# Row maxima of attention pairs 1 to 7 in two parts, spread differently over the first steps

## The chip, the core and the metric

The kernel runs on one core of one Trainium2 chip. The metric is the device time of one execution in microseconds (us), the median of several runs. Five engines work side by side on a core and meet only through semaphores: PE (TensorE, matmuls into PSUM), DVE (VectorE), ACT (ScalarE), POOL (GpSimd) and SP (SyncE), which here does nothing but issue DMAs. Each engine runs its own list of instructions strictly in order: an instruction that waits holds back all that stand behind it on the same engine.

## The reference, cut to what matters

```python
def _attn_ref(q, k, v):                       # 8 batches, 8 heads, 1152 positions, 64 wide
    q_pool = q.reshape(B, H, S // 2, 2, D).mean(axis=3)
    scores = scale * np.matmul(q_pool, k.transpose(0, 1, 3, 2))
    scores = scores - np.max(scores, axis=-1, keepdims=True)
    attn = np.exp(scores)
    attn = attn / (np.sum(attn, axis=-1, keepdims=True) + 1e-09)
    return np.matmul(attn, v)

def _moe_ref(x, modality_id, w_gate, modality_bias, w1, w2):   # 4608 tokens, 8 experts
    logits = x @ w_gate + modality_bias[modality_id]
    e_idx = np.argmax(logits, axis=1)
    ...                                       # softmax weight of the chosen expert
    for e in range(E):
        h = np.maximum(x[mask] @ w1[e], 0.0)
        out[mask] = gate_w[mask, None] * (h @ w2[e])
```

The attention output is the input of the mixture of experts. The change lies in the attention alone.

## The kernel before, in words

**Pairs and steps.** The 64 heads are worked two at a time: 32 pairs, which the code and this text number p = 0 to 31 (the "pairs 2 to 8" of the change's title are p = 1 to 7). A pair takes NSTEP = 18 steps, so the attention is one loop over 576 steps t in `attention`; then `experts` runs the expert blocks. The order of instructions on each engine is exactly the order in which this loop writes them (a manual schedule). ORD says in which order a step writes its parts: "s" writes one bank of scores (432 columns: a product with B1 at L1051, one with B2 at L1052, then the exponential on ACT at L1053), "v" one chunk of the products of probabilities with values (L1110 to L1112), "M" one piece of the row maxima, "X" extra pieces of the row maxima by a rule, "F" and `ends` what was put off to this step.

**Row maxima.** The softmax needs the largest score of each query before the exponentials. `maxpass(p)` makes rough products of queries (tile QB) and keys (tile hi) for this alone: for each of 9 blocks of 128 queries two products of 512 keys (L984), each followed by a `tensor_reduce` on DVE (L985), and for every four blocks one product of the last 128 keys (L992, L993). A PSUM tile `pm` holds a product until DVE has reduced it; there are three. That makes 18 L984 products and 21 pieces per pair. `row` then takes the maximum of the parts (DVE, L935, tile m), turns it with PE (L949) into a row, scales it (DVE, L958, tile mr) and copies it by a DMA of SP (L959) into row D of B2, where the score products (L1052) pick it up as one more term. In a pair the first head (j = 0, the pair's steps 0 to 8) needs queries 0 to 575 and the second head (j = 1, steps 9 to 17) queries 576 to 1151. A pair in TWO_ROWS sends its maxima as two rows, blocks 0 to 4 and blocks 5 to 8, and its first head waits for the first of them only; other pairs send one row of 9 blocks ahead of their first step.

**How many pieces.** `mxq` is the queue of started maxima. M takes one piece per step. X takes three per step while t < T_F, one per step while t < X_ALL = 8, and after that one in every step with t % X_IN == 0 or whenever two pairs stand in the queue (every fourth step from t = 105 on).

**Queues around it.** SP issues, in program order, the loads of raw queries, keys and values (L756, L757, L761), the copies that place a pair's operands (L739: QB, B1, B2), the rows (L959), the zero rows of B2 (L1209) and the transposes of finished outputs (L1094). A DMA's semaphore is one of eight that SP uses in turn. POOL makes sums and casts of queries (L771, L780, tile qh), low parts (L818, tile lo), high parts of values (L911 to L918, VH) and, from p = 4 on, issues the DMA that loads the keys cast to f16 (L795 in `load_hi`, tile hi). The load of pair p + 3's raw queries and keys (`load_kq`) and the transposes of outputs (`turns`) are issued in `put`, right behind the row that ends with block 8.

Of the kernel before, what the change touches and what calls it, by code (L numbers as in the profile page):

```python
# [40 lines left out]
NSTEP = 2 * NKC  # L41
# [19 lines left out]
T_RT = (20, 35, 43, 61)  # L61
D2 = (1, 0, 0, 0, 3)
T_K2 = 0
T_F = 7
T_P2 = 1
T_P1 = 8
T_M1 = 5
# [4 lines left out]
T_CAST = -36  # L72
# [2 lines left out]
T_PLACE = -17  # L75
T_REST = -13
ST = 2
T_LV = (-24, -34, -36)
VS0 = 4
V1 = (9, 11, (14, 15), 18, (18, 19))  # L80
LOWS0 = (((0, 1152, 'A', 2), (1152, 1728, 'D', 3)),)
# [65 lines left out]
ORD = ('NvJMvsvMsvXF', 'JvvsMvvXFvv', 'vFvvsJvXv')  # L147
FIRST = (0, 1)
T_PRE = 1
TWO_ROWS = (1,)  # L150
X_ALL = 8
X_SOME = 105
X_IN = 3
T_MX2 = -23
T_MX3 = -23
FIN = 0
# [541 lines left out]
def attention(tc, ctx, att, ident, npairs, xpool, on_two, on_split, on_scale, jobs, side, set_pm, started, ahead, hip, own_port):  # L698
# [39 lines left out]
    def move(o, i):  # L738
        nc.sync.dma_start(out=o, in_=i)  # L739
# [35 lines left out]
    def split_qh(p):  # L775
        s = st[p]
        qh = s["qh"]
        made.add((p, "qh"))
        if p > 1:
            (nc.gpsimd if QH_POOL else nc.vector).tensor_copy(qh, s["q"][:, 0:SQ])  # L780
        else:
            nc.scalar.copy(qh, s["q"][:, 0:SQ])
        if p > 1:
            place_qb(p)

    def place_qb(p):
        qh = st[p]["qh"]
        for j in range(2):
            r = slice(j * D, (j + 1) * D)
            move(QB[p % 2].rearrange("p u n -> p (u n)")[r, j * SQ:(j + 1) * SQ], qh[r])  # L790
# [140 lines left out]
    def row(p, mp, u0, u1):  # L931

        n = u1 - u0
        m9 = sm.tile([P, 9], F32, name="m9")
        nc.vector.tensor_reduce(m9[:, 0:n], mp[:, u0:u1], op=ALU.max, axis=AX.X, negate=True)  # L935

        def first_row():
            nc.vector.tensor_scalar(first_m[:, :, D], m9[:, 0:n], 1.0 / ROW, 16.0 * math.log(PSC) / ROW, op0=ALU.mult, op1=ALU.add)
            for v0, v1, pt, copy in ((0, 3, small(), nc.scalar.copy), (3, n, some(0), nc.vector.tensor_copy)):
                for v in range(v0, v1):  # L940
                    nc.tensor.matmul(pt[0:D + 1, (v - v0) * P:(v - v0 + 1) * P], first_m[:, v], ident16, start=True, stop=True, skip_group_check=True)
                copy(B2[0][D:D + 1, 2 * S + v0 * P:2 * S + v1 * P], pt[D:D + 1, 0:(v1 - v0) * P])
            made.add((p, f"row{u1}"))

        def finish():
            if p == 0 and u0 == 0:
                return first_row()
            pt = some(0) if p else small()
            nc.tensor.transpose(pt[0:n, 0:P], m9[:, 0:n], ident)  # L949
            if now[0] > NSTEP:  # L950
                later_end(FD, lambda: put(pt))
            else:
                put(pt)

        def put(pt):
            mr = sm.tile([9, P], F16, name="mr", bufs=1)
            made.add((p, f"row{u1}"))
            nc.vector.tensor_scalar(mr[0:n], pt[0:n, 0:P], 1.0 / ROW, 16.0 * math.log(PSC) / ROW, op0=ALU.mult, op1=ALU.add)  # L958
            nc.sync.dma_start(out=B2[p % 2][D:D + 1, 2 * S + u0 * P:2 * S + u1 * P], in_=mr[0:n])  # L959
            if ahead and p == npairs - 1:  # L960
                for i in FIRST:
                    ahead[2](i, room[i])
            while turns:
                turns.pop(0)()
            if ahead and p == npairs - 1:
                for i in range(len(FIRST), NF):
                    ahead[2](i, room[i])
            if 0 < p < npairs - 3 and u1 == 9:
                load_kq(p + 3)
        return finish  # L970

    def maxpass(p, mp=None):

        s = st[p]
        need(p, *(("qh", "hi0", "hi1") if p else ()))
        u0 = 0 if mp is None else 5
        two = p in TWO_ROWS
        rest = []
        if mp is None:
            mp = sm.tile([P, 9, 3], F32, name="mp")  # L980
        for u in range(u0, 9):
            for t in range(2):
                pm = ps_max.tile([P, 512], F32, name="pm")
                nc.tensor.matmul(pm, QB[p % 2][:, u], s["hi"][:, t * 512:(t + 1) * 512], start=True, stop=True)  # L984
                nc.vector.tensor_reduce(mp[:, u, t:t + 1], pm, op=ALU.max, axis=AX.X)  # L985
                yield
            rest.append(u)
            if len(rest) == 4 or u == 8 or two and u == 4:
                n = len(rest)
                pm = ps_max.tile([P, 512], F32, name="pm")[:, 0:n * P].rearrange("p (n k) -> p n k", n=n)  # L990
                for i, v in enumerate(rest):
                    nc.tensor.matmul(pm[:, i], QB[p % 2][:, v], s["hi"][:, 1024:S], start=True, stop=True, skip_group_check=True)  # L992
                nc.vector.tensor_reduce(mp[:, rest[0]:u + 1, 2], pm, op=ALU.max, axis=AX.X)  # L993
                rest.clear()
                if two and u == 4:
                    later_end(FIN if now[0] > NSTEP else 1, row(p, mp, 0, 5))
                    u0 = 5
                yield
        later_end(FIN if now[0] > NSTEP else 3 if p == 0 else 2, row(p, mp, u0, 9))

    def first_max(p):

# [145 lines left out]
    now, flushed = [0], [-1]  # L1148
    free = [0] * NR
    todo, at_end = {}, {}  # L1150
    mxq, pvq, scq = [], [], []
# [4 lines left out]
    def later_end(n, fn):  # L1156
        at_end.setdefault(now[0] + n, []).append(fn)

    def at(t, p, fn, end=True):
        if 0 <= p < npairs:  # L1160
            (at_end if end else todo).setdefault(max(t, 0), []).append(fn)
# [6 lines left out]
    def ends(t):  # L1168
        while at_end.get(t):
            at_end[t].pop(0)()  # L1170

    def advance(q, n):
        for _ in range(n):
            while q and next(q[0], DONE) is DONE:
                q.pop(0)
# [105 lines left out]
    for p in range(npairs):  # L1281
        b = NSTEP * p
        go = lambda t, f, *a, p=p, b=b, **k: at(b + t, p, lambda: f(p, *a), **k)
        if p > 1:
            d = D2 if p == 2 else (0,) * 5
            if p < 4:
                go((T_K2, T_K3)[p - 2] - b, load_kq, end=False)
            go(T_SPLIT[p > 2] + d[0], split_q)
            go(T_QH[p > 2] + d[1], split_qh)
            if p > 3:  # L1290
                go(T_CAST, load_hi)
            else:
                for i in range(2):
                    go(T_HI[i] + d[2], split_hi, i)
            for i in range(3):
                go(T_LO[p > 2][i] + d[3], split_lo, i)
            go({2: T_MX2, 3: T_MX3}.get(p, T_MAX), lambda p: mxq.append(maxpass(p)), end=False)
            go(T_PLACE + (T_P2 if p == 2 else 0), place, end=False)
            if p > 2:
                go(T_REST, place_rest, end=False)  # L1300
            go(T_LV[max(0, min(p, 4) - 2)], load_v)
        elif p:
            go(T_P1 - b, place, end=False)
            go(T_M1 - b, lambda p: mxq.append(maxpass(p)), end=False)
            go(T_LV[max(0, min(p, 4) - 2)], load_v)
        sq, power_, vh, vs, vl = (T_SQ, T_POW, T_VH, T_VS, T_VL) if p > 1 else V1
        if p == 0:
            at(VS0, 0, lambda: shifted(0))
            continue
        if p == 1:  # L1310
            go = lambda t, f, *a, p=p: at(t, p, lambda: f(p, *a))
        go(sq, square)
        go(power_, power)
        for i, t in enumerate(vh):
            go(t, values, i, False)
        go(vs, shifted)
        for i, t in enumerate(vl):
            go(t, values, i, True)
# [14 lines left out]
    for t in range(NSTEP * npairs):  # L1333
        p, c18 = divmod(t, NSTEP)
        now[0] = t
        if jobs and c18 in JOBS:
            running.append(jobs.pop(0))
        for a in ORD[t % len(ORD)]:
            if a == "J":
                running[:] = [g for g in running if next(g, DONE) is not DONE]  # L1340
            elif a == "F":
                flush(t)
            elif a == "M":
                advance(mxq, 1)
            elif a == "X":
                advance(mxq, 3 if t < T_F else 1 if t < X_ALL or t % (X_IN if t < X_SOME else 4) == 0 or len(mxq) > 1 else 0)
            elif a == "N":
                scq.append(scores(p, *divmod(c18 // 3, 3)))
            elif a == "s":
                advance(scq, 1)  # L1350
            elif a == "v":
                advance(pvq, 2 if len(pvq) > 2 else 1)
        ends(t)
        if side and t >= wait:
            r = next(side[0], DONE)
            if r is DONE:
                side.pop(0)
            else:
                wait = t + (r or 1) if (r or 1) > 0 else NSTEP * npairs + r
# [484 lines left out]
```

## Time and profile before

| | |
|---|---|
| median of 3 runs | 1108.47 us (1107.31 to 1111.22) |
| the profiled execution's own time | 1107.82 us |
| its span, first to last instruction | 1106.1 us |
| PE, DVE, ACT, POOL busy, share of the span | 99%, 86%, 79%, 41% |
| granted clock of PE, mean | 1.00 |

Everything below is read from the one profiled execution. A timeline row gives the start in us from the span's start, the time taken, engine, line, operation, output and inputs, shape, how many instructions are merged in the row, and in brackets the idle time of the engine before it and what ended it. The matmuls of PE are pipelined, and the printed time of one is longer than its share of the engine; what a matmul costs, and what a wait costs, is read from the distance between starts.

### The profile page before, as it was taken

To read this page: it belongs to the slowest core of one execution; us is meant where nothing else is said; L and a number is where in the kernel's file an instruction comes from. 1 tells how busy PE (TensorE), PEld (TensorE's weight loads), DVE (VectorE), ACT (ScalarE), POOL (GpSimd) and SP (SyncE) were. 2 spreads that over 40 slices of the span, in tenths; PEclk is the share of its full clock that TensorE was granted. 3 is DMA by queue.
4 is the path that set the end of the run, shared out by engine and by line. 5 is a ranking of instruction groups with operands and counts; after the bars stand their busy time and mean duration, and the time that the engine had idled before them with its cause. 6 is when DMAs were issued, how large, how long until landed. Compare 5 with 4: busy or idle time off the path is not lost. (4 is left out here: it accounts for less than half of the span.)

```text
span 1106.1 us, 36764 instructions
## 1 busy us (share of the span) xinstructions
PE 1093.6 (99%) x15133; PEld 811.7 (73%) x15133; DVE 952.3 (86%) x1902; ACT 876.7 (79%) x1391; POOL 451.5 (41%) x485
## 2 busy tenths in 40 slices
PE   8999999999999999999999999999999999999998
PEld 4777777777777777777777777876677667667666
DVE  8999999999999999999999999789987756756751
ACT  6899999999999999899999999876556655655652
POOL 8765434454444455445545453132123121121112
PEclk9999999999999999999999999999999999999999
DMA  8788867878677778677786765699989999899970
GB/s 255 182 204 206 206 174 185 206 183 206 170 210 200 182 198 204 161 198 192 202 200 170 215 152 128 188 293 308 279 257 239 335 286 275 269 283 266 286 207 33
DMA packets 178356, 237.59 MB, mean 215 GB/s; under 512 B 91555, under 2 KB 127027, under 8 KB 178180
## 3 DMA queue, kind: packets, MB, share of 16 engines
q1 hardware_dynamic: 168004, 207.12, 67.4%
q0 software_dynamic: 10176, 28.05, 11.6%
q8 instruction: 120, 1.97, 0.8%
q14 instruction: 56, 0.46, 0.1%
HBM read 158.43 MB, written 18.99 MB: 160 GB/s over the span
## 5 line engine op out<-in xcount | busy, mean ns | idle before, releaser
L1053 ACT ACTIVATE Pe<-psc 128x432 int32<-128x432 f32 x768 | 383.0, 525 | 53.4 <-PE psc L1052 34.3
L985 DVE TENSOR_REDUCE mp<-pm 128x1 f32<-128x512 f32 x566 | 372.7, 684 | 12.1 <-PE pm L984 5.6
L1111 PE MATMUL xp<-VS,Pl 128*128 128x65 f16 x2880 | 374.7, 194 | 0.0
L1110 PE MATMUL xp<-VH,Pe 128*128 128x65 f16 x2880 | 373.1, 193 | 0.0
L1112 PE MATMUL xp<-vl,Pe 128*128 128x64 f16 x2880 | 370.6, 192 | 0.0
L1111 PEld LDWEIGHTS <-Pl 128*128 128x128 f16 x2880 | 267.3, 97 | 86.4
L1051 PE MATMUL psc<-B 128*128 128x432 f16 (+2 forms) x1152 | 302.0, 286 | 0.0
L1052 PE MATMUL psc<-B 128*128 128x432 f16 (+5 forms) x1152 | 301.9, 286 | 0.0
L1110 PEld LDWEIGHTS <-Pe 128*128 128x128 f16 x2880 | 271.2, 97 | 40.4 <-issue 1.9
L1112 PEld LDWEIGHTS <-Pe 128*128 128x128 f16 x2880 | 268.8, 98 | 0.0
L1034 ACT ACTIVATE Pl<-Pe 128x1152 f16<-128x1152 uint16 x186 | 216.5, 1164 | 5.9
L984 PE MATMUL pm<-hi,QB 128*128 128x512 f16 x566 | 213.9, 379 | 2.6 <-DVE mp L985 1.5
L1498 PE MATMUL ph<-xpart,w1l 128*128 128x256 f16 x544 | 148.4, 273 | 0.0
L1496 PE MATMUL ph<-xpart,w1h 128*128 128x256 f16 x544 | 148.3, 273 | 0.0
L1497 PE MATMUL ph<-xpart,w1h 128*128 128x256 f16 x544 | 148.3, 273 | 0.0
L818 POOL TENSOR_TENSOR lo<-rawk,hi 128x576 f16<-128x576 f32 (+1 forms) x68 | 83.3, 1228 | 152.5 <-DVE Pl L1036 130.4
L1052 PEld LDWEIGHTS <-B 128*128 128x128 f16 (+1 forms) x1152 | 112.1, 97 | 21.7
L1051 PEld LDWEIGHTS <-B 128*128 128x128 f16 x1152 | 111.4, 97 | 6.2 <-DMA B<-lo 0.6
L918 POOL TENSOR_SCALAR VH<-rawv,scales 128x512 f16<-128x512 f32 (+1 forms) x63 | 109.1, 1733 | 15.6 <-DVE Pl L1036 13.8
L1502 DVE SCALAR_TENSOR_TENSOR hl<-ph,hh 128x512 f16<-128x512 f32 x72 | 49.7, 691 | 74.8 <-ACT hh L1501 64.9
L1501 ACT ACTIVATE hh<-ph 128x512 f16<-128x512 f32 x72 | 42.9, 596 | 83.8 <-PE ph L1498 83.8
L1614 PE MATMUL po<-w2l,hh 128*128 128x512 f16 x280 | 106.2, 379 | 0.0
(327 smaller groups left out, 1888.3 us busy)
## 6 DMA issues: line engine op xcount, KB each, us to landing
w2r<-in_w_dram SPq DMA_DIRECT2D x72, 512.0 KB
w1r<-in_w_dram SPq DMA_DIRECT2D x68, 512.0 KB
rawv<-in_att_dram SPq DMA_DIRECT2D x32, 576.0 KB
B<-hi SPq DMA_DIRECT2D x128, 144.0 KB
rawq<-in_att_dram SPq DMA_DIRECT2D x31, 576.0 KB
rawk<-in_att_dram SPq DMA_DIRECT2D x31, 576.0 KB
B<-qh SPq DMA_DIRECT2D x128, 72.0 KB
B<-lo SPq DMA_DIRECT2D x64, 144.0 KB
```

Source lines behind the costliest of these rows:

```text
L984: nc.tensor.matmul(pm, QB[p % 2][:, u], s["hi"][:, t * 512:(t + 1) * 512], start=True, stop=True)
L985: nc.vector.tensor_reduce(mp[:, u, t:t + 1], pm, op=ALU.max, axis=AX.X)
L1034: nc.scalar.activation(low, rest, AF.Copy, scale=LOW)
L1051: nc.tensor.matmul(o, b1[:, ks], b1[:, qs], start=True, stop=False, skip_group_check=True)
L1052: nc.tensor.matmul(o, b2[:, ks], b2[:, qs], start=False, stop=True, skip_group_check=True)
L1053: nc.scalar.activation(Pe[:, D + x0:D + x1], pt, AF.Exp, scale=1.0 / 16)
L1110: nc.tensor.matmul(out, Ph[:, qs], vh[:, c, j, 0:D + 1], start=c == 0 and g == 0, stop=False, skip_group_check=True)
L1111: nc.tensor.matmul(out, Pl[:, qs], vs[:, c, j, 0:D + 1], start=False, stop=False, skip_group_check=True)
L1112: nc.tensor.matmul(out[:, 0:D], Ph[:, qs], vl[:, c, j], start=False, stop=c == NKC - 1, skip_group_check=True)
L1496: nc.tensor.matmul(o, hi[:, c, fs], xh[:, :, c], start=c == 0, stop=False)
L1497: nc.tensor.matmul(o, hi[:, c, fs], xl[:, :, c], start=False, stop=False)
L1498: nc.tensor.matmul(o, lo[:, c, fs], xh[:, :, c], start=False, stop=c == 3)
```

## The change

Seven edits, in the numbers that set the order and in three lines of code:

- TWO_ROWS goes from (1,) to 1 to 7, so p = 2 to 7 send two rows instead of one. That is one L935, L949, L958 and L959 more for each.
- T_F goes from 7 to 2, X_IN from 3 to 4, and the catching up while two pairs are queued holds only from t = 105 on: fewer pieces of maxima in the first steps, more of them later.
- A row of a two-row pair is turned by PE two steps after its maxima were taken. Before, it was one step for the first row of p = 1, and the same step for p = 2 to 7.
- The QB copies of p = 2 move from step 10 to T_QB2 = 15, and its load of raw values from step 12 to step 16.
- `load_hi` of p = 4 to 9 is issued five steps later, at 31 steps ahead of the pair instead of 36.

```diff
-T_F = 7
+T_F = 2
...
-T_LV = (-24, -34, -36)
+T_QB2 = 15
+T_LV = (-20, -34, -36)
...
-TWO_ROWS = (1,)
+TWO_ROWS = tuple(range(1, 8))
 X_ALL = 8
 X_SOME = 105
-X_IN = 3
+X_IN = 4
...
             nc.scalar.copy(qh, s["q"][:, 0:SQ])
-        if p > 1:
+        if p == 2:
+            at(T_QB2, p, lambda: place_qb(p))
+        elif p > 2:
             place_qb(p)
...
                 if two and u == 4:
-                    later_end(FIN if now[0] > NSTEP else 1, row(p, mp, 0, 5))
+                    later_end(2 if now[0] > NSTEP else 1, row(p, mp, 0, 5))
                     u0 = 5
                 yield
-        later_end(FIN if now[0] > NSTEP else 3 if p == 0 else 2, row(p, mp, u0, 9))
+        later_end(3 if p == 0 else 2 if two or now[0] <= NSTEP else FIN, row(p, mp, u0, 9))
...
             if p > 3:
-                go(T_CAST, load_hi)
+                go(T_CAST + (5 if p - 2 in TWO_ROWS else 0), load_hi)
...
             elif a == "X":
-                advance(mxq, 3 if t < T_F else 1 if t < X_ALL or t % (X_IN if t < X_SOME else 4) == 0 or len(mxq) > 1 else 0)
+                advance(mxq, 3 if t < T_F else 1 if t < X_ALL or t % (X_IN if t < X_SOME else 4) == 0 or len(mxq) > 1 and t >= X_SOME else 0)
```

From p = 7 on the order on every engine is the old one, but for the DMAs of hi of p = 8 and 9. Line numbers of the changed kernel are up to three higher than those of before. Three places follow.

DVE in steps 3 to 12 of p = 0, from the first row of maxima (mr) on. Pl is the low part of the exponentials, one such row in three steps; mp, m and mr are the maxima; half, scales and both belong to the values. Before:

```order
L958 TENSOR_SCALAR mr<-pj 4x128
L985 TENSOR_REDUCE mp<-pm 128x1 x8
L1036 TENSOR_SCALAR Pl_118<-Pe_117 128x576
L993 TENSOR_REDUCE mp<-pm 128x4
L985 TENSOR_REDUCE mp<-pm 128x1 x2
L993 TENSOR_REDUCE mp<-pm 128x1
L935 TENSOR_REDUCE m_569<-mp 128x5
L985 TENSOR_REDUCE mp<-pm 128x1
L1036 TENSOR_SCALAR Pl_120<-Pe_119 128x576
```

And now:

```order
L961 TENSOR_SCALAR mr<-pj 4x128
L988 TENSOR_REDUCE mp<-pm 128x1 x4
L1039 TENSOR_SCALAR Pl_118<-Pe_117 128x576
L988 TENSOR_REDUCE mp<-pm 128x1 x4
L996 TENSOR_REDUCE mp<-pm 128x4
L1039 TENSOR_SCALAR Pl_120<-Pe_119 128x576
L988 TENSOR_REDUCE mp<-pm 128x1
```

Four reductions stand between the first row and the next Pl where there were eight, and the first row of p = 1 (m of 5 blocks) has moved behind the next Pl.

SP around the rows of p = 1. B_1_113 is the B2 of p = 1, into which its two rows (mr) go; B_0_111 and B_923 take the operands of p = 2, QB_114 the queries of p = 3; wg, bias and idt are constants of the expert stage. Before:

```order
L959 DMA B_1_113<-mr 1x5x128
L761 DMA rawv<-in_att_dram 128x1152
L959 DMA B_1_113<-mr 1x4x128
L756 DMA rawq<-in_att_dram 128x1152
L757 DMA rawk<-in_att_dram 128x1152
L739 DMA B_0_111<-qh 64x576 x2
L739 DMA B_923<-qh 64x576 x2
L739 DMA B_923<-lo 64x576 x2
L739 DMA B_0_111<-lo 64x1152 x2
L739 DMA B_923<-hi 64x1152 x4
L190 DMA wg<-in_w_gate_dram 128x4x8
```

And now, further down the same list:

```order
L762 DMA rawv<-in_att_dram 128x1152
L740 DMA QB_114<-qh 64x576 x2
L962 DMA B_1_113<-mr 1x4x128
L757 DMA rawq<-in_att_dram 128x1152
L758 DMA rawk<-in_att_dram 128x1152
L1212 DMA B_0_111<-zero 48x8x432
```

The second row of p = 1 (4 blocks) stood ahead of the twelve copies that place p = 2; now it stands behind these twelve, the three constants, the values of p = 3 and the two QB copies of p = 3.

POOL, the f16 keys of p = 4. VH is the high part of the values of p = 3, qh the cast of the queries of p = 4. Before:

```order
L795 DMA hi<-in_att_dram 128x1152
L895 COPY both<-scales 64x1
L918 TENSOR_SCALAR VH_123<-rawv,scales 128x8x64
L918 TENSOR_SCALAR VH_123<-rawv,scales 128x10x64
L780 CAST qh<-rawq 128x576
```

And now:

```order
L898 COPY both<-scales 64x1
L921 TENSOR_SCALAR VH_123<-rawv,scales 128x8x64
L921 TENSOR_SCALAR VH_123<-rawv,scales 128x10x64
L781 CAST qh<-rawq 128x576
L798 DMA hi<-in_att_dram 128x1152
```

The DMA of hi now stands behind both VH instructions and the cast of qh; the same for p = 5 to 9.

## Rows read from the trace of the kernel before

**Rows 1.** The page, part 1: engines, busy us, share of the span, instructions.

```profile
PE 1093.6 (99%) x15133; PEld 811.7 (73%) x15133; DVE 952.3 (86%) x1902; ACT 876.7 (79%) x1391; POOL 451.5 (41%) x485
```

**Rows 2.** Busy time by stretch: stretch, length, engines with counts, clock, DMA share, GB/s.

```profile
16.80:42.40 25.60, 23.55 (x313) 16.13 (x311) 24.53 (x52) 21.48 (x37) 21.50 (x18) 1.00 0.75 214
110.30:131.80 21.50, 21.50 (x377) 16.70 (x373) 20.84 (x44) 20.03 (x37) 9.86 (x10) 1.00 0.78 168
197.40:218.70 21.30, 21.30 (x376) 16.63 (x373) 20.43 (x44) 20.04 (x37) 9.49 (x9) 1.00 0.79 171
```

**Rows 3.** Timeline of p = 0, three places, PE and one row of DVE.

```profile
23.04 0.19 PE L1112 MATMUL xp<-vl,Pe 128*128 128x64 f16 x1
23.07 4.85 DVE L985 TENSOR_REDUCE mp<-pm 128x1 f32<-128x512 f32 x8
...
23.79 0.38 PE L984 MATMUL pm<-hi,QB 128*128 128x512 f16 x1 [0.56 <-DVE mp L985]
...
25.24 0.72 PE L984 MATMUL pm<-hi,QB 128*128 128x512 f16 x2
...
26.18 0.38 PE L984 MATMUL pm<-hi,QB 128*128 128x512 f16 x1 [0.22 <-DVE mp L985]
26.40 0.19 PE L1110 MATMUL xp<-VH,Pe 128*128 128x65 f16 x1
...
32.40 0.19 PE L1112 MATMUL xp<-vl,Pe 128*128 128x64 f16 x1
...
32.89 0.38 PE L984 MATMUL pm<-hi,QB 128*128 128x512 f16 x1 [0.30 <-DVE mp L985]
```

**Rows 4.** Timeline of p = 1, three places on PE.

```profile
54.70 0.23 PE L1052 MATMUL psc<-B 65*128 65x144 f16 x1
...
55.30 0.38 PE L992 MATMUL pm<-hi,QB 128*128 128x128 f16 x4 [0.37 <-DVE mp L985]
...
59.37 0.28 PE L949 MATMUL pm<-ident,m 128*9 128x128 f32 x1
...
59.48 0.19 PE L1110 MATMUL xp<-VH,Pe 128*128 128x65 f16 x1
...
60.37 0.19 PE L1112 MATMUL xp<-vl,Pe 128*128 128x64 f16 x1
...
60.76 0.39 PE L984 MATMUL pm<-hi,QB 128*128 128x512 f16 x1 [0.20 <-DMA QB<-qh]
```

**Rows 5.** Timeline of SP, 41 to 58 us: DMA issues.

```profile
41.61 0.66 SPq L959 DMA_DIRECT2D B<-mr  x1
...
43.33 2.58 SPq L739 DMA_DIRECT2D B<-qh  x4
...
55.65 2.39 SPq L739 DMA_DIRECT2D QB<-qh  x2
```

**Rows 6.** Timeline of POOL: low keys of p = 2, queries of p = 3 and p = 8.

```profile
35.61 1.47 POOL L818 TENSOR_TENSOR lo<-rawk,hi 128x576 f16<-128x576 f32 x1 [3.69 <-DMA QB<-qh]
...
52.09 0.66 POOL L780 CAST qh<-rawq 128x576 f16<-128x576 f32 x1
...
159.75 0.66 POOL L780 CAST qh<-rawq 128x576 f16<-128x576 f32 x1
```

**Rows 7.** Timeline of PE: the second head of p = 1 begins; maxima of p = 8 begin.

```profile
52.87 0.35 PE L1052 MATMUL psc<-B 65*128 65x432 f16 x1
...
168.49 0.38 PE L984 MATMUL pm<-hi,QB 128*128 128x512 f16 x1
```

**Rows 8.** Timeline of the start: a small copy and the weight load that waits for it.

```profile
13.43 0.59 SPq L739 DMA_DIRECT2D B<-lo  x1
...
15.69 0.10 PEld L1051 LDWEIGHTS <-B 128*128 128x128 f16 x1 [0.62 <-DMA B<-lo]
```

**Rows 9.** Line L795, the DMA of hi on POOL: last row of its view.

```profile
DMA to landing us min/median/max: 4.5/6.6/9.1
```

**Rows 10.** Busy time by stretch, the end of the span (columns as in rows 2).

```profile
1103.00:1106.10 3.10, 0.00 (x0) 0.00 (x0) 0.00 (x0) 0.00 (x0) 0.00 (x0) 0.83 0.17 53
```

## The prediction, made before the changed kernel was timed

> **What bounds the kernel now.** I read the page's part 1 first: PE is busy for 99% of the span [rows 1]. A busy PE isn't PE at its peak, so next I took the busy time by stretch of one pair each. p = 0 takes 25.60 us, p = 4 21.50 us and p = 8 21.30 us [rows 2]; odd pairs hold a little other work and differ. So the loss of the first pairs is a few us, and nothing that the change touches lies behind p = 8. In p = 0 DVE is busy for 24.53 of 25.60 us [rows 2]: there DVE sets the pace, while in p = 8 PE works without a break (21.30 of 21.30) and DVE has 0.9 us of room. Then I went through the timeline of the first pairs and looked for places where the distance between two starts on PE is longer than the first of them costs. A value product costs 0.03 us (23.04 would have been followed at 23.07), a product of 512 columns 0.22 us (26.18 to 26.40) [rows 3]. What is left over is the wait.
>
> **The waits that can go.** In p = 0 the maxima of p = 1 come four to a step, and eight reductions take DVE 4.85 us, 0.61 each [rows 3]; PE finds no free PSUM tile. From 23.04 to 23.79 that is 0.75 less 0.03, so 0.72; from 25.24 to 26.18 it is 0.94 less two products, 0.50; from 32.40 to 32.89 0.49 less 0.03, 0.46 [rows 3]. Together 1.68 us. In the changed order only four reductions stand there, PE and DVE come to terms, and I count all three as gone. Waits of the same kind before 20 us stay, since the steps before t = 2 are as they were. In p = 1 the product at 55.30 starts 0.60 after one of 144 columns that costs 0.06 (0.22 x 144/512): 0.54 of wait for DVE. The one at 60.76 starts 0.39 after a value product, 0.36 of wait for the QB copies of p = 3, whose first use comes one third of a pair later now [rows 4]. I count both, 0.90 us. Further waits of p = 3 to 6, about 0.3 us each, I count neither as gains nor as losses: DVE gets work there. Sum of the gains: 2.6 us.
>
> **What is added.** Six rows more: six turns on PE, each 59.48 - 59.37 = 0.11 us [rows 4], all on the path, since PE is the bound: 0.66 us. The six extra pairs of small DVE instructions lie beside PE in pairs with room (0.9 us in p = 8) [rows 2], so nothing, unless that room is gone (third rival). The number of maxima products is the same; those moved out of p = 0 are paid later, at the same price. Turning a row two steps later removes a wait of PE for DVE at the turn, and costs nothing by itself. Without new waits the change is worth 0.66 - 2.6 = -1.9 us.
>
> **The new wait.** The second row of p = 1 is needed by the first L1052 of its second head, which starts at 52.87 [rows 7]. Before, SP issued this row at 41.61 [rows 5], eleven us ahead. In the new order it is the last of nineteen DMAs, and directly ahead of it stand the two QB copies of p = 3, which need qh of p = 3. SP can't issue the row before POOL has made that qh, however early DVE has the maxima. When is that? POOL works from 35.61 to 52.09 + 0.66 = 52.75 almost without a break [rows 6]. Its start hangs on the cast of p = 2's keys on ACT, which stands between exponentials and so moves with PE: 1.7 us earlier for the waits, and 0.6 for three products that now stand later. So qh of p = 3 is there at about 50.4. Two QB copies on SP at 2.58/4 = 0.64 each [rows 5] make 51.7 for the issue of the row. From issue to landing I take 2.3 us, from the small copy issued at 13.43 that a weight load waited for until 15.69 [rows 8]: 54.0. And PE arrives earlier than before: 52.87 - 1.7, less six maxima products of 0.22 that the new order puts behind this place: 49.9. PE waits 4.1 us, and nothing can fill it, since PE runs in order. The bounds: if the row landed as soon as its issue ended (0.66 at 41.61 [rows 5]) the wait would be 2.4; if it took as long as the QB copies of p = 3, issued at 55.65 and waited for until 60.76, 5.1 us [rows 4, 5], it would be 6.9. Twelve copies of p = 2 stand ahead as well, but they start when p = 0 has read its B2 for the last time and have ten us until then, so POOL decides and not they. A wait below nothing is excluded: PE can't run ahead of its order.
>
> A row of this trace says that small copies take 2.3 us and that the extra ones cost SP 0.64 us each, beside PE [rows 5, 8]. The Trainium skill, "DMA: Bandwidth & Descriptors", gives each DMA a fixed cost of about 2.0 us and advises to coalesce small transfers ("Rules for kernel authors"), which speaks against cutting a row in two. By its 2.0 us the wait would be 3.8 instead of 4.1; the sum hardly moves, because here the place in the queue weighs more than the copy.
>
> **The sum.** -1.9 + 4.1 = +2.2, less a little because DVE and POOL catch up during that wait: +2.0 us. The profiled execution took 1107.82, so 1109.8 on its scale; it stands 0.65 below the median of the three runs, and on the median's scale the forecast is 1108.47 + 2.0 = 1110.5 us.
>
> **Rivals.** First, the row is there in time: qh of p = 3 comes earlier than I think, or PE arrives later because waits of p = 0 remain. For it speaks that POOL's chain starts from a cast whose releaser the profile names as a DMA (35.61 [rows 6]), so it may move differently; against it, that POOL has seventeen us of work there (35.61 to 52.75) that nobody takes away. Then the whole is -1.9: 1106.6 us.
>
> Second, and slower: the keys of p = 4 to 9 come late. Their DMA now waits on POOL behind qh of the same pair. For p = 8 qh ends at 160.4 [rows 6], and its first maxima product starts at 168.49 [rows 7], 8.1 us later; issue to landing takes 6.6 us in the median and 9.1 at most [rows 9]. At the median nobody waits, at the maximum PE waits 1.0 us or more, in up to six pairs. It decides from a landing time of about 8 us on. Two copies of raw queries and keys and two transposes, which are issued behind the same later rows, crowd the DMA at the same time. Four pairs at 1.0 us on top of the forecast: 1114.5 us.
>
> Third, DVE becomes the bound in p = 3 to 5. The pieces moved out of p = 0 to 2 go there, up to two more per pair, 1.2 us, with the second row's 0.3: 20.84 + 1.5 = 22.3 where p = 4 takes 21.50 [rows 2, 3]. Against it: reductions back to back cost 0.61, and busy time counts isolated ones longer. Price 0.8 a pair in three pairs: 1112.9 us.
>
> Fourth, the clock falls. After PE's last work, at the end of the span, the granted clock of a stretch without PE work is 0.83, partly below the upper level of 2.4 GHz [rows 10]; it is 1.00 in all stretches of the first pairs [rows 2]. A wait of 4 us might do the same in the middle. If the next 4 us then ran at 1.2 GHz, that would cost 2 us: 1112.5 us. The Trainium skill, "TensorE: Matmul & The Clock Gate" ("HAM oscillation"), says just this of matmul loops that wait for DMA; no stretch of this trace has one inside the work.
>
> **How the numbers follow.** Chances: forecast 0.50, row in time 0.22, late keys 0.14, DVE 0.08, clock 0.06. Differences under 0.3% (3.3 us, about what a measurement of this kernel can tell from no change) count as the same: 1105.1 to 1111.8. Of the forecast's half, the longer waits (6.9 gives +5) are slower, 0.08, and 0.41 stay within; of the row in time half, 0.11, may reach faster where further waits go as well; late keys 0.11 of 0.14, DVE 0.06 of 0.08 and clock 0.05 of 0.06 are slower. With 0.01 of the forecast faster: faster 0.12, same 0.58, slower 0.30. The range runs from 1105.5 (row in time, and 1 us of the further waits gone) to 1114.5 (the long wait, or late keys).
>
> **What would show it.** In the changed kernel's timeline: no wait above 0.2 us at maxima products between 22 and 34 us; the second row of p = 1 (L962) issued by SP right behind the QB copies, which start when POOL's L781 of p = 3 ends; an idle PE of some 4 us in front of the first L1055 of p = 1's second head, ended by the DMA of mr. p = 0 should take about 23 us instead of 25.60, p = 1 some 3 us longer than before. If PE passes that place without a wait, the forecast is wrong and the first rival holds; if PE waits for hi at the first maxima product of p = 6 to 9, the second.

## The result and the profile after

The changed kernel takes 1122.77 us in the median (1118.90 to 1124.29), the kernel before on the same chip 1109.72: 1.0114 times as long, with a 95% interval of 1.0081 to 1.0148. It is slower by 12 to 13 us and lies far outside the predicted range. The profiled execution took 1123.21 us, its span is 1121.5. Three kernels below had one or two executions in a slow state, from 1.25 to 2 times as long, and every median and ratio leaves these out.

The same stretches as in [rows 2] for the changed kernel, from the first exponential of one pair to that of the next (p = 0 to 8; length, then PE, PEld, DVE, ACT, POOL busy, granted clock, DMA share, GB/s):

```profile
16.50:45.20 28.70, 22.97 (x327) 16.21 (x325) 23.31 (x48) 21.33 (x36) 26.39 (x21) 1.00 0.77 208
45.20:69.10 23.90, 23.22 (x372) 17.50 (x372) 20.43 (x44) 21.27 (x37) 8.95 (x8) 0.93 0.59 141
69.10:93.70 24.60, 21.87 (x371) 16.63 (x368) 23.11 (x49) 20.43 (x36) 16.12 (x27) 0.98 0.81 190
93.70:119.40 25.70, 24.66 (x408) 18.82 (x405) 22.13 (x48) 20.69 (x34) 12.67 (x20) 0.95 0.72 162
119.40:141.60 22.20, 22.12 (x381) 17.10 (x379) 21.30 (x48) 20.43 (x36) 9.42 (x10) 1.00 0.74 187
141.60:164.20 22.60, 22.32 (x389) 17.20 (x386) 21.93 (x48) 20.25 (x34) 9.80 (x10) 1.00 0.73 186
164.20:189.80 25.60, 23.23 (x374) 17.64 (x371) 21.65 (x48) 20.52 (x36) 10.84 (x10) 0.93 0.74 179
189.80:212.30 22.50, 22.50 (x403) 17.58 (x401) 21.20 (x46) 20.25 (x36) 10.55 (x11) 1.00 0.84 226
212.30:233.60 21.30, 21.30 (x374) 16.64 (x371) 20.41 (x44) 20.05 (x36) 9.43 (x9) 1.00 0.78 177
```

And the four pairs of the kernel before that answer to the long ones and aren't in [rows 2] (p = 1, 2, 3, 6):

```profile
42.40:66.40 24.00, 23.42 (x402) 17.98 (x401) 22.89 (x49) 21.16 (x38) 15.11 (x12) 1.00 0.79 210
66.40:88.10 21.70, 21.70 (x376) 16.77 (x373) 21.01 (x45) 20.08 (x35) 14.89 (x27) 1.00 0.96 181
88.10:110.30 22.20, 22.06 (x394) 17.19 (x391) 21.31 (x45) 20.12 (x35) 13.06 (x21) 1.00 0.77 220
153.60:175.30 21.70, 21.56 (x376) 16.66 (x372) 20.75 (x44) 20.20 (x36) 9.37 (x9) 1.00 0.76 174
```

From p = 8 on nothing differs (21.30 in both). Four pairs carry the loss: p = 0 +3.1, p = 2 +2.9, p = 3 +3.5, p = 6 +3.9. In the stretches of p = 1, 2, 3 and 6 the clock is below 1.00, which it is in no stretch of a pair shown of the kernel before. What PE waited for between 20 and 200 us in the changed kernel (waiting line, what it waited for, us in all, times, longest):

```profile
PE pm L879 <- ACT vl L873: 4.5, 1, 4.5
PE psc L1055 <- DMA B<-mr: 2.4, 1, 2.4
PE pm L987 <- DVE mr L961: 2.4, 1, 2.4
PE pm L288 <- DMA xt<-x: 1.0, 1, 1.0
PE pm L987 <- DVE mp L988: 0.8, 3, 0.3
```

Four single waits make 10.3 us. These are the idle times that the profile prints; counted from start to start, as the expectations below do, the long ones are some 0.2 us longer. Before, the list had three small waits (0.4 us and less) and this line:

```profile
PE pm L984 <- DVE mp L985: 1.1, 3, 0.6
```

**The first wait, 4.5 us at the start of p = 1.** SP, ACT and PE of the changed kernel around it:

```profile
36.48 0.77 SPq L962 DMA_DIRECT2D B<-mr  x1
37.37 2.18 SPq L740 DMA_DIRECT2D QB<-qh  x2
39.60 0.58 SPq L762 DMA_DIRECT2D rawv<-in_att_dram  x1
...
44.05 1.16 ACT L873 ACTIVATE vl<-rawv 128x1152 f16<-128x1152 f32 x1 [5.52 <-DMA rawv<-in_att_dram]
...
45.36 0.16 PE L879 MATMUL pm<-ss,ones 128*128 128x1 bf16 x1 [4.49 <-ACT vl L873]
```

The sum of squares of p = 2's values (L873, ACT) stands one step behind the place to which the change moved their load (T_LV -20, T_SQ -19). The load is issued at 39.60, behind the two QB copies, ACT waits for it 5.52 us, and PE waits for ACT.

**The second, 2.4 us at the start of p = 3.** SP, DVE and PE:

```profile
75.95 0.45 SPq L757 DMA_DIRECT2D rawq<-in_att_dram  x1
76.44 1.11 SPq L758 DMA_DIRECT2D rawk<-in_att_dram  x1
...
81.19 6.19 SPq L740 DMA_DIRECT2D B<-hi  x4
82.94 0.27 DVE L961 TENSOR_SCALAR mr<-pm 5x128 f16<-5x128 f32 x1
87.48 0.53 SPq L249 DMA_DIRECT2D xs<-x  x1
88.11 0.77 SPq L962 DMA_DIRECT2D B<-mr  x1
...
93.12 0.52 PE L1055 MATMUL psc<-B 128*128 128x432 f16 x1 [2.41 <-DMA B<-mr]
```

The four hi copies take SP 6.19 us, since it waits 3.7 us there for the landing of the raw keys issued at 76.44. DVE has written the first row of p = 3 by 83.2, 7.5 us before PE comes to it; SP issues it only at 88.11, right behind the copy of xs (87.48), and PE gets it at 93.12, 5.0 us after its issue. So this row isn't late from its maxima: its time goes in SP's list and in the landing. A row of about this size without such a neighbour had 2.0 us to the end of the wait for it (52.02 to 54.03, in the first experiment). The Trainium skill, "DMA: Bandwidth & Descriptors" ("Queues, rings and completion order"), has a DMA's semaphore land only after every earlier write of the same DMA engine; 5.0 us behind xs and 2.0 us elsewhere agree with that, without excluding that the crowded DMA alone makes the difference.

**The third, 2.4 us at the end of p = 6.** SP, DVE and PE:

```profile
173.15 0.27 DVE L961 TENSOR_SCALAR mr<-pm 5x128 f16<-5x128 f32 x1
...
178.82 0.53 SPq L249 DMA_DIRECT2D xs<-x  x1
179.45 6.50 SPq L962 DMA_DIRECT2D B<-mr  x2
...
184.98 0.28 DVE L961 TENSOR_SCALAR mr<-pm 4x128 f16<-4x128 f32 x1 [3.11 <-DMA B<-mr]
...
185.31 0.59 PE L987 MATMUL pm<-hi,QB 128*128 128x512 f16 x1 [2.37 <-DVE mr L961]
```

The second row of p = 7 must be written into the one buffer mr, out of which the DMA of its first row still reads. That row was written at 173.15 and issued at 179.45, again behind the hi copies and xs. DVE waits 3.11 us for its DMA, reduces nothing, and PE has no free pm.

The fourth wait, 1.0 us at 106.31, is for a transpose of finished outputs (xt), which SP issues behind the rows; no run takes it by itself.

**The clock.** Behind each of these three waits PE runs at 1.2 GHz, half the upper level, for a while. What follows the first, as a whole and in two parts (columns as above, the clock third from the end):

```profile
45.20:49.00 3.80, 3.64 (x34) 2.26 (x33) 1.88 (x7) 3.12 (x8) 3.80 (x3) 0.57 0.97 224
45.20:48.40 3.20, 3.04 (x27) 1.88 (x27) 1.46 (x7) 2.95 (x7) 3.20 (x3) 0.50 0.98 225
48.50:49.00 0.50, 0.50 (x8) 0.30 (x6) 0.33 (x1) 0.17 (x1) 0.50 (x1) 1.00 1.00 235
```

One product of the maxima in each part, in the timeline of PE:

```profile
46.73 0.61 PE L987 MATMUL pm<-hi,QB 128*128 128x512 f16 x1
...
48.72 0.38 PE L987 MATMUL pm<-hi,QB 128*128 128x512 f16 x1
```

The first has half the clock around it and takes 0.61 us, the second 1.00 and 0.38. The clock lost over a pair follows from its mean: 0.93 of 23.9 us is 0.14 of it at the half, 3.3 us, so 1.7 lost; in the same way 1.3 for p = 3 and 1.8 for p = 6, 4.8 at most together, a little of it inside the waits. So 10.3 of waits, up to 4.8 of clock, 0.7 for the six turns, less 0.8 of waits in p = 0: 15.0, where the nine stretches differ by 217.1 - 201.9 = 15.2.

### The profile page after: what moved, and what is told of

The parts are those of the page before. It is cut to its first block, busy times and chain, and to the rows that moved or that the text cites. A ratio compares the mean times of both kernels' runs of the same rounds, so it can differ in the third digit from the quotient of the medians.

```text
span 1121.5 us, 36827 instructions
## 1 busy us (share of the span) xinstructions
PE 1098.3 (98%) x15139; PEld 815.0 (73%) x15139; DVE 953.6 (85%) x1914; ACT 879.1 (78%) x1391; POOL 447.9 (40%) x485
## 5 line engine op out<-in xcount | busy, mean ns | idle before, releaser
L1113 PEld LDWEIGHTS <-Pe 128*128 128x128 f16 x2880 | 272.3, 98 | 50.4 <-issue 12.6
L1618 PE MATMUL po<-w2h,hl 128*128 128x512 f16 x280 | 106.1, 379 | 0.0
```

The costliest lines, as they stand in the source:

```text
L1113: nc.tensor.matmul(out, Ph[:, qs], vh[:, c, j, 0:D + 1], start=c == 0 and g == 0, stop=False, skip_group_check=True)
```

## The experiments

The ratio is to the kernel before, run beside it on the same chip; the changed kernel stands at 1.0114.

**Three waits, three causes?** First each wait's neighbour alone.

```diff
-T_LV = (-20, -34, -36)
+T_LV = (-24, -34, -36)
```

> The changed kernel with one number put back: the load of p = 2's raw values four steps earlier (T_LV -24 instead of -20). Theory 'three causes': PE's wait of 4.5 us at the first work of p = 1 is ended by the square on ACT, which waits for this load; without it that wait goes (-4.7 us) and with it the stretch behind it that ran at half the clock (-1.7 us): about 6.4 us less than the changed kernel, 1116.4 us, and every later wait stays. Rival 'the wait is passed on': the power of p = 2's values, made late, also held POOL and so the QB copies of p = 3 and the second row of p = 1; with everything earlier the row is the next that is late and PE waits for it in p = 1's second head, up to the 4.1 us of the forecast: only about 2.3 us less, 1120.5 us. A DMA wait at the first L1055 of p = 1's second head tells them apart.

Measured: 1120.79 us, 1.0104 (1.0082 to 1.0126): of 6.4 expected us about 1 came. The first wait is gone, and PE waits in p = 1's second head instead, in SP's and PE's rows of this kernel:

```profile
50.80 1.13 SPq L740 DMA_DIRECT2D QB<-qh  x2
52.02 0.67 SPq L962 DMA_DIRECT2D B<-mr  x1
...
54.03 0.52 PE L1055 MATMUL psc<-B 65*128 65x432 f16 x1 [2.91 <-DMA B<-mr]
```

That is the wait of the forecast, at its place and with its cause. In the changed kernel it was hidden, since PE came five us later. The wait was passed on. The one for the row of p = 3 is there too, with 3.1 us.

```diff
-            mr = sm.tile([9, P], F16, name="mr", bufs=1)
+            mr = sm.tile([9, P], F16, name="mr", bufs=2)
```

> The changed kernel with two buffers for the tile mr instead of one. Theory 'three causes': the second row's scaling on DVE waits 3.1 us for the DMA of the first row, which still reads the only mr; DVE then reduces nothing and PE waits 2.4 us for pm at the end of p = 6. With two buffers DVE doesn't wait: -2.5 us and -1.7 us for the slow stretch behind it, 4.2 us less than the changed kernel, 1118.6 us; the waits at 45, 93 and 106 us stay. Rival: DVE was only the messenger and the late first row itself would stop PE at p = 7's first scores; then at most 1 us is gained.

Measured: 1119.44 us, 1.0090 (1.0069 to 1.0112). DVE no longer waits for the buffer, but 1 us later PE waits 1.9 us for the first row itself, at the first scores of p = 7, as the rival has it. The gain, over 2 us, is more than the rival allows, but the first wait, which the edit doesn't touch, is also 1.2 us shorter in this execution.

```diff
-                go(T_CAST + (5 if p - 2 in TWO_ROWS else 0), load_hi)
+                go(T_CAST, load_hi)
```

> The changed kernel with the DMA of the f16 keys (hi, p = 4 to 9) issued where it was before, five steps earlier. Theory 'three causes': at 76 to 77 us the loads of raw queries, raw keys and hi start together and take up to 10.5 us to land; SP waits 3.7 us for one of them, the first row of p = 3 is issued at 88.1 and PE waits 2.6 us for it at the first L1055 of p = 3. With hi earlier the three loads are apart: -2.6 and -1.7 us for the slow stretch, 4.3 us less than the changed kernel, 1118.5 us. Rival: the row is late because it stands behind the loads and the copy of x (xs) in SP's list and is made two steps later, whatever lands when: the wait stays within 0.5 us and the time within 1 us.

Measured: 1120.22 us, 1.0100 (1.0077 to 1.0123). The 2.4 us at p = 3 are gone, but two waits for other rows make 2.5 us, two for transposes 1.4, and 1.6 stand at p = 1's second head, which the profile puts down to a load of values issued just ahead of that row. Passed on again. The reverse edit, in the kernel before:

```diff
-                go(T_CAST, load_hi)
+                go(T_CAST + (5 if p < 10 else 0), load_hi)
```

> The kernel before with the DMA of hi for p = 4 to 9 issued five steps later and nothing else. The prediction's second rival: PE waits for hi at the first maxima of these pairs, or SP for the crowded loads: +1 to +4 us. The forecast's view, that the rest of the room hides it: within 0.5 us of before.

Measured: 1108.56 us, 0.9990 (0.9980 to 1.0001). By itself the later load costs nothing.

The edits of the first three together:

> The three edits together: values of p = 2 earlier, two mr buffers, hi earlier. If the three causes are independent the gains add up: 6.4 + 4.2 + 4.3 = 14.9 us less than the changed kernel, 1107.9 us, about the time of before; what is then left over against before is the gain and the price of the changed maxima alone (-2.6 + 0.7 by the prediction, so down to 1106.6). If waits are passed on, clearly more than 1110.

Measured: 1117.04 us, 1.0076 (1.0049 to 1.0103): of 14.9 expected us some 4 came. In the profiled execution (1120.99) PE still waits 3.4 us at p = 1's second head, 1.0 in p = 2, 1.1 for hi copies of p = 6 and 2.0 before p = 7.

**The pacing.** The catching up put back in the changed kernel, then that and the three edits:

```diff
-... or len(mxq) > 1 and t >= X_SOME else 0)
+... or len(mxq) > 1 else 0)
```

> The changed kernel with the catching up put back: one piece of maxima per step whenever two pairs are queued, from the first step on. Theory 'late maxima': the rows are late because the pacing makes the maxima as late as they may be, and then every hitch of SP or DMA reaches PE. With the catching up the rows of p = 2 to 7 are there earlier: the waits at 93, 106 and 185 us and the slow stretches of two of them go, the one for the values at 45 stays: 9 to 10 us less than the changed kernel's 1122.8, so about 1113. Rival 'place in the queue': the rows stay behind the loads in SP's list and the DMAs stay crowded, so the waits stay or move: within 2 us of the changed kernel.

Measured: 1116.71 us, 1.0080 (1.0067 to 1.0093): some 4 us less, between the two forecasts. The wait for the row of p = 3 is gone, two of 2.6 us together for mr and 2.1 for the values stay, and eight for reductions make 3.8.

> The changed kernel with four edits: values of p = 2 earlier, two mr buffers, hi earlier, and the catching up of the maxima put back. Theory 'late maxima': the three single causes and the pacing are all there is; what is left of the change is thinner first steps and two rows: 1107 to 1109 us. Rival 'place in the queue': rows still wait behind loads: 1113 us or more.

Measured: 1113.79 us, 1.0048 (1.0034 to 1.0062). By the number the rival is right, but not by its mechanism: PE waits for no row in this execution. From p = 3 to p = 7 it takes 109.70 us, the kernel before 109.30, the changed one 118.60: there the loss is gone but for five pairs' second rows at 0.11 each. What is left lies in p = 0 to 2, with 2.1 us for QB of p = 2 and 2.6 for reductions. A fifth edit:

```diff
-T_QB2 = 15
+T_QB2 = 10
```

> The kernel with four edits (values earlier, two mr buffers, hi earlier, catching up) and as a fifth the QB copies of p = 2 at step 10 again. PE waited 2.2 us at 42.6 for just these copies. If their step decides, that wait goes: 2 to 3 us less than 1114.1, about 1111.5. If they wait anyway until PE has read the old queries of p = 0 for the last time, which the thin first steps put off, the wait stays within 0.5 us.

Measured: 1112.09 us, 1.0034 (1.0021 to 1.0048), and the clock of the profiled execution is 1.00 throughout. The wait for QB is gone, 1.5 us for the second row of p = 1 take its place. The first three pairs and the next five of this kernel:

```profile
16.50:41.70 25.20, 22.50 (x307) 15.55 (x305) 23.38 (x49) 21.42 (x37) 22.93 (x18) 1.00 0.81 226
41.70:67.50 25.80, 23.50 (x405) 18.01 (x404) 23.23 (x50) 21.25 (x37) 12.84 (x10) 1.00 0.55 139
67.50:91.40 23.90, 22.54 (x377) 17.11 (x375) 22.72 (x49) 20.38 (x36) 14.87 (x27) 1.00 0.85 195
91.40:201.20 109.80, 109.71 (x1925) 85.44 (x1923) 104.88 (x229) 100.25 (x170) 54.13 (x58) 1.00 0.79 202
```

p = 0 is 0.4 us shorter than before, p = 1 and 2 are 1.8 and 2.2 longer. PE waits 2.8 us for reductions in all (1.5 before) and 2.2 for rows (none before). That would fit maxima which, taken from the first steps, meet a DVE with 22.9 of 24.0 us of work already; but the run with the old first steps further down takes just as long.

**The first steps.** All of the change, but T_F as before:

```diff
-T_F = 2
+T_F = 7
```

> The changed kernel with T_F 7 again and all else as changed (pacing without catching up, QB and values of p = 2 late, one mr, hi late). Theory 'late maxima': the 14 or so pieces more in the first steps bring every later row forward, so the waits at 45, 93 and 185 us get shorter or go, though each edit that was blamed for one is still in: 1113 or less. Theory 'three causes', each by itself: the waits stay, 1120 or more.

Measured: 1115.51 us, 1.0072 (1.0057 to 1.0086). What PE waited for in it from 20 to 200 us:

```profile
PE pm L987 <- DVE mr L961: 3.0, 2, 1.6
PE pm L987 <- DMA QB<-qh: 2.8, 2, 1.5
PE pm L987 <- DVE mp L988: 1.6, 4, 0.6
```

The values of p = 2 are still loaded one step ahead of their square, and ACT still waits for them, but 1.18 us instead of 5.52, and PE for neither them nor a row. The only mr buffer and QB still cost. By the time, 4.7 us less than the changed kernel (from the ratios), it lies between the two theories. So the waits at p = 1 and p = 3 needed the thin first steps as well as what each was put down to; the wait for mr did not.

Now the parts alone, in the kernel before. The first steps thinned (T_F 2, catching up kept), and thinned a little (T_F 6):

> The kernel before with T_F 2 instead of 7 alone: fewer maxima in the first steps, caught up in the steps after, since two queued pairs still advance every step. Theory (the prediction's gain): the waits for DVE between 22 and 34 us (1.7 us) go and nothing else changes: about 1.7 us less than before, if the maxima that move meet a DVE with room. Rival: p = 0 has no room anywhere (DVE 24.5 of 25.6 us), the waits only move: within 0.5 us of before; or the second row of p = 1 comes later and PE waits for it: slower.

Measured: 1112.26 us, 1.0037 (1.0024 to 1.0050): slower, as the last of the rivals has it. p = 0 takes 24.10 us instead of 25.60, nearly the gain predicted, and p = 1 takes 28.30 instead of 24.00: two waits for rows make 1.9 us, and DVE has 25.86 us of work in it where it had 22.89. In the profiled execution (1114.08) the first exponential comes 2.6 us late, behind a wait of 4.0 us from 13 to 17 us that the edit doesn't touch.

> The kernel before with T_F 6 instead of 7: two pieces of maxima fewer in the first steps, and SP's list keeps its order. If the thinning is good while no row moves behind loads, the wait of 0.7 us at 23 us goes and the kernel is up to 1 us faster than before; if DVE in p = 0 has no room for the two pieces later either, within 0.5 us of before.

Measured: 1114.11 us, 1.0059 (1.0036 to 1.0083), worse than either forecast. Two pieces fewer, and the second row of p = 1 is issued at 45.52 (before: 41.61 [rows 5]). All that stands behind it in SP's list shifts with it, and PE waits at the next place, for QB of p = 3:

```profile
45.52 0.66 SPq L959 DMA_DIRECT2D B<-mr  x1
...
59.83 1.11 SPq L739 DMA_DIRECT2D QB<-qh  x2
...
65.70 0.39 PE L984 MATMUL pm<-hi,QB 128*128 128x512 f16 x1 [4.20 <-DMA QB<-qh]
```

Evenly spread, with nearly the same number of pieces by step 9:

```diff
-advance(mxq, 3 if t < T_F else 1 if t < X_ALL or ...
+advance(mxq, 3 if t < 2 else 2 if t < 9 else 1 if t < X_ALL or ...
```

> The kernel before with the first maxima spread evenly: three extra pieces per step in steps 0 and 1, then two per step up to step 8, instead of three up to step 6 and one at step 7. The sum by step 9 is nearly the same, so every row after the first comes when it did and SP's list keeps its order. If the wait of 0.7 us at 23 us can go without making anything late, up to 1 us less than before: 1107. If a row that comes a step later matters (as with T_F 6): 1111 or more.

Measured: 1110.09 us, 1.0012 (1.0002 to 1.0021). PE's waits for DVE fall by 0.4 us, the one for QB of p = 3 rises from 0.2 to 1.4. The same with p = 1's maxima begun a step earlier (T_M1 4, two per step up to step 7) took 1115.03 us, 1.0046 (1.0033 to 1.0058), with 3.7 us for QB and 1.6 for a row. None of these beats the kernel before.

**Two rows and their turns.** TWO_ROWS 1 to 7 alone, in the kernel before:

> The kernel before with TWO_ROWS 1 to 7 alone: six rows more, each 0.11 us on PE, nothing moved otherwise: +0.7 us by the prediction. Rival 'rows collide': the second of two rows waits for the only mr until the first row's DMA has landed, or stands behind the loads that the first row's put no longer triggers; then waits of 1 to 3 us at the ends of p = 1 to 6, +2 to +8 us.

Measured: 1112.51 us, 1.0042 (1.0029 to 1.0055). Neither the buffer nor the queue did it:

```profile
PE pm L949 <- DVE m L935: 4.2, 7, 0.8
```

Each row is turned right behind its maximum, and PE waits for that. (The profiled execution, at 1115.56, has the same late start as that with T_F 2 alone.) The delay of two steps is there to remove this wait. Taken out of the changed kernel:

```diff
-                    later_end(2 if now[0] > NSTEP else 1, row(p, mp, 0, 5))
+                    later_end(FIN if now[0] > NSTEP else 1, row(p, mp, 0, 5))
...
-        later_end(3 if p == 0 else 2 if two or now[0] <= NSTEP else FIN, row(p, mp, u0, 9))
+        later_end(FIN if now[0] > NSTEP else 3 if p == 0 else 2, row(p, mp, u0, 9))
```

> The changed kernel with the rows turned as before (no two steps in between for p = 2 to 7, the second row of p = 1 at once). Two theories on the 2.6 us for which PE waits for the first row of p = 3 at 93 us. 'Delay': the row comes two steps (some 2.5 us) later than it could, and that is the wait; without the delay the waits at 93 and 185 us go, but PE waits for DVE at the turns (0.8 us each in the kernel with two rows alone, 13 turns): about 2 us less than the changed kernel, 1121. 'Queue': the row is issued late because SP waits for landings ahead of it; then the waits at 45, 93 and 185 us stay and the waits at the turns come on top: 1126 or more.

Measured: 1121.83 us, 1.0115 (1.0090 to 1.0140). PE's waits for what it turns are 8.1 us in ten places, while those at p = 3 and p = 7 are gone: the two steps buy as much as they cost. For p = 7 this shows the delay at work. Without it SP issues the first row here, ahead of the lo and hi copies and of xs, where the changed kernel has it at 179.45, behind them:

```profile
170.65 0.76 SPq L962 DMA_DIRECT2D B<-mr  x1
```

For p = 3 it doesn't. That row stands behind the hi copies and xs without the delay too (written at 80.63, issued at 84.52); what is gone is SP's wait of 3.7 us in these copies. In the kernel of the last experiment below, which keeps the delay and the changed kernel's order, SP doesn't wait there either, the row is issued at 83.77, and PE doesn't wait for it.

Two rows with the delay, two mr buffers and X_IN 4, but first steps, catching up, hi, QB and values as before:

> The changed kernel with the first steps, the catching up, the place of hi, of p = 2's queries and of its values all as before, and two mr buffers: so the kernel before with two rows for p = 2 to 7, turned two steps later, two mr buffers and X_IN 4. Theory 'first steps': what costs is the thinning of the first steps, which makes the maxima late; then this is before plus six turns: 1108 to 1109.5. Rival 'rows': the second row and its place in SP's list cost by themselves: 1111 or more.

Measured: 1113.29 us, 1.0035 (1.0023 to 1.0047): the rival, by its number. PE waits 2.3 us for reductions (1.5 before), 1.3 for a row (none before) and 1.1 for QB (0.2 before); with 0.7 for the six turns that is the 3.7 us between the medians. This kernel differs from the one with five edits in T_F alone, and the two take the same, 1.0035 and 1.0034. So thin first steps cost something only where the rest of the change is in place or the kernel is otherwise the old one; with the five edits they are free, and what remains is in the two rows, their delay and X_IN 4. No run has the delay or X_IN by itself.

**The clock.**

```diff
         pt = some(1)
+        if p == 2:
+            for _ in range(17):
+                nc.tensor.matmul(pt, QB[0][:, 0], s["hi"][:, 0:512], start=True, stop=True)
         nc.tensor.matmul(pt[:, 0:1], ones.broadcast_to([P, P]), s["ss"], start=True, stop=True)
```

> The changed kernel with 17 products of 512 columns, whose results nobody reads, put on PE in front of the power of p = 2's values, where PE waits 4.5 us: 17 x 0.22 = 3.7 us, so they fit into the wait and cost nothing by themselves. Theory 'the wait lowers the clock': the stretch behind the wait runs at 1.00 instead of half the clock, and p = 1 is 1.7 us shorter (22.2 us instead of 23.9 from its first exponential to that of p = 2); the other waits and their slow stretches stay: about 1121. Rival: the clock falls for another reason (time or work before): the stretch at half the clock stays and the time is that of the changed kernel, 1122.8.

Measured: 1119.17 us, 1.0075 (1.0046 to 1.0103). The products and the power behind them in this kernel's timeline:

```profile
42.07 3.83 PE L881 MATMUL pm<-hi,QB 128*128 128x512 f16 x17
45.74 0.17 PE L882 MATMUL pm<-ss,ones 128*128 128x1 bf16 x1
```

And the stretch that follows, in its view by stretch:

```profile
45.70:49.50 3.80, 3.80 (x65) 2.83 (x63) 2.85 (x10) 1.97 (x5) 3.72 (x3) 1.00 0.74 150
```

The clock stays at 1.00, and 65 instructions of PE fit into a stretch as long as the one that held 34 before. So it is the idle PE that lowers the clock here. From the power to the first exponential of p = 2 it is 22.3 us (45.74 to 68.0) instead of 23.7 (45.36 to 69.1): 1.4 of the 1.7 us expected. The rest of the gain is not from this place: the wait for the row of p = 3 isn't there in this execution.

## Why the prediction was wrong, point by point

- **The step that failed** is the part on what is added, up to "Without new waits the change is worth 0.66 - 2.6 = -1.9 us". What the change puts later is priced there at its work alone, and at nothing for whatever waits for it: the moved maxima "are paid later, at the same price", a turn two steps later "costs nothing by itself", and the load of p = 2's values, which goes from step 12 to 16, one step ahead of the square that needs it, isn't priced at all. In place of nothing the changed kernel shows waits of 4.5 us for these values, 2.4 for the row of p = 3, 2.4 for the buffer mr and 1.0 for a transpose, and up to 4.8 us of clock behind the first three. The thin first steps alone, forecast at -1.7, cost 4.1 (1.0037). No single term is the whole: with the values put back the kernel is still at 1.0104, with the old first steps at 1.0072, with five edits at 1.0034.
- **The new wait** of 4.1 us was real, but of the kernel with the values put back: there the row is issued at 52.02 (forecast 51.7) and PE waits until 54.03 (54.0), 2.9 us, since PE came a good us later than I had it. In the changed kernel the row is issued at 51.69, just as forecast, but PE comes to it only at 56.30, behind the first wait. So the chain through POOL and SP was right, and its place in the sum wrong.
- **The turn two steps later**, which "costs nothing by itself", failed for p = 7: two steps more put its first row behind the copies in SP's list, and the one buffer mr, which a second row makes into a wait, was not looked at. The row of p = 3 was late for another reason, SP's wait for the raw keys.
- **The gains:** the three waits of p = 0 did go (1.1 us of printed idle time; one of 0.3 for something else came); the pair gains 1.5 with T_F alone (1.7 counted), and in the changed kernel it takes 28.70 us, 24.2 without the first wait, where about 23 was forecast. The 0.9 of p = 1 did not: two waits of 0.4 each stand there again. With T_F alone the maxima come back as 3 us of DVE work in p = 1.
- **The turns:** six at 0.11; five pairs from p = 3 to 7 are 0.5 longer in the repaired kernel, as counted.
- **Rivals.** Late keys: in the changed kernel PE never waits for hi, and the later load alone costs nothing; but the crowded DMA of that rival held SP 3.7 us. DVE: p = 4 and 5 are 0.7 and 0.8 longer, the price given, but DVE isn't the bound there (21.30 of 22.20 us busy, PE 22.12), so the agreement is luck; PE has moved products and turns to do. The clock: given 0.06 and 2 us once; it fell three times. The forecast itself held a wait of 4 us, so this price belonged into its own sum. The Trainium skill, "TensorE: Matmul & The Clock Gate" ("HAM oscillation"), has matmul loops that wait for DMA fall back to the lower clock, and the trace agrees, with 0.57 in 45.20 to 49.00.
- **The range** took one wait and one rival at a time. What happened were several waits at once, at places where an in-order list had little slack. That late maxima are their one cause isn't shown: the old first steps or the catching up, put back alone, take off about 4.7 and 3.8 of 12.6 us (from the ratios), and the row of p = 3 was written in time.

Open: the first wait differs between kernels whose lists are equal up to there: 4.5 us in the changed one, 3.3, 2.2 and 1.1 in those with two mr buffers, earlier keys and no delay. Ahead of it SP waited 2.4, 2.3, 1.9 and 1.0 us for the landing of raw keys, in the same order; why that landing takes longer in one execution than in another wasn't settled, and the same holds for SP's wait at p = 3. Open too is how the last 0.35% divide between the rows, their delay and X_IN. Each kernel has one trace, so a wait that is there in one and not in another may also be chance.

## What to carry to other kernels

Price every moved instruction against the one that needs it: list its new step, its reader's step, and the landing time between them. When work is put off, follow all that hangs on its end, above all on an in-order queue that issues DMAs, where one late entry holds back everything behind it. Mending the wait that shows, alone, mostly shows the next one. Before calling a result late, look when it was ready, when it was issued and when it landed: the row of p = 3 was ready at 83.2, issued at 88.1 and there at 93.1.

## What the runs showed of the hardware

The granted clock fell to the half (1.2 GHz) in the middle of the work. Counted over all traces, start to start on PE, it did so behind all fifteen waits of 2.5 us or more and behind four of nine between 2.0 and 2.4. Of the shorter ones it did so behind two, 1.8 and 1.9 us, both at about 14 us, where the work begins. Products whose results nobody reads, put into a wait of 4.5 us, kept it at 1.00. Up to 1.8 us were lost each time in the changed kernel; three other traces hold 0.50 for 6.7 us at a stretch behind a wait in the middle (43.10 to 49.80 with two mr buffers).
